# Splitting four head groups instead of two at the end of the first layer, with the schedule's settings chosen anew

## Chip, core and metric

The kernel runs on one core of a Trainium2 chip. The metric is the device time of one execution in microseconds; the engines are TensorE (PE), VectorE (DVE), ScalarE (ACT), GpSimd (POOL) and SyncE (SP), which issues the DMAs.

## What is computed

Two layers, each an attention block and a gated feed-forward block with residual additions, on one sequence of 2048 tokens of width 512, with 32 heads of width 16. The weights of both layers are the same.

```python
def _A_ref(x, wqkv, wo):                       # S=2048, D=512, H=32, Dh=16
    q, k, v = split(x @ wqkv)                  # each (H, S, Dh)
    scores = einsum("bhqd,bhkd->bhqk", q, k) * Dh ** -0.5
    p = softmax(scores)
    return merge(einsum("bhqk,bhkd->bhqd", p, v)) @ wo

def _B_ref(x, w_gate, w_up, w_down):           # hidden width 1792
    return (gelu(x @ w_gate) * (x @ w_up)) @ w_down

x = x + _A_ref(layernorm(x), wqkv, wo)
x = x + _B_ref(layernorm(x), w_gate, w_up, w_down)
x = x + _A_ref(layernorm(x), wqkv, wo)
x = x + _B_ref(layernorm(x), w_gate, w_up, w_down)
```

## The kernel before

**Units.** The queries of a layer are cut into blocks: four of 512 tokens in layer 0, three of 512 and two of 256 in layer 1. Heads are taken in groups of four. One *unit* is one block and one head group. A unit is worked in two passes. The first pass multiplies Q and K, tiles of 128 queries by 512 keys, and takes the maximum of each row (L2440 on PE, L2455 on DVE); a unit of 512 queries has 64 such tiles, and a layer 2048. The maxima go through six small POOL instructions (L1538 to L1543), a transposition on DVE (L1549) and four small DMAs into a spare row of Q's tile (`QT<-MT`). The second pass multiplies K and Q the other way round, so that the maximum is subtracted by the product itself (L2318), takes exponentials on ACT (L2290, table load before the first one after a GELU) and multiplies them with V on PE (L2343), all units in one PSUM bank; a column of ones in V yields the sums. At a unit's end, `nrm` copies the bank on ACT (L1591, tile `ACCS`), and POOL takes the reciprocal and scales (L1597, L1602).

**Folded tiles.** For a part of the first pass, POOL subtracts two quarters of K (L2020, tile `KD`); PE multiplies Q by the difference, ACT takes the positive part (L2270), and one custom instruction on DVE (L2450) then covers two tiles. `want_fold` chooses this when the second pass is close behind the first.

**Dense products.** When all head groups of a block are done, the block's output projection, the layer norm, the three feed-forward products, the next layer's layer norm and its Q, K and V follow. Most are recorded at one helper line (L1235 on PE, `evac` at L1250 on DVE or L1252 on ACT). `x_add` reads a projection out (ACT L1615 and POOL L1617, or DVE L1610). In most blocks the GELU is formed from a tanh, by `gate`, on POOL and ACT (L1743 to L1753), since tanh and the exponential are in one table; in the last block of a layer the gate products are read out by ACT's own GELU function (L1922), which needs a table load, and no exponentials are taken meanwhile. Up products are multiplied in by `L1940`/`L1942`, `L1958`/`L1960` or on DVE (L1952).

**The end of a layer.** The last block of a layer is split: its last `SPL0` head groups in layer 0 (`SPL` in layer 1) are worked by halves of the block, first all of them for half 0, then all of them for half 1, so that half 0's dense products can begin before half 1 is done. Half 0 of layer 0 (256 tokens) takes the tanh way, half 1 the GELU function. The first pass of layer 1 may begin earlier, on the three first quarters of K, for six units; the last quarter of K needs both halves' feed-forward blocks.

```python
k = (SPL if la == NL - 1 else SPL0) if qi == len(sizes) - 1 else 0
if k:
    blocks += [(la, qi, t0, n // 2), (la, qi, t0 + n // 2, n // 2)]
for g in range(NG - k):                     # whole units of the last block
    units.append((la, b, t0, n, g))
for h in range(2 if k else 0):              # then half 0, then half 1
    for g in range(NG - k, NG):
        units.append((la, b + h, t0 + h * n // 2, n // 2, g))
```

**The order of work.** A loop in Python, when the program is built, decides what each engine's stream holds next. It keeps an estimated clock for each engine; in each turn it compares the time at which the next reduction and the next exponential can be fed, and puts dense pieces in between as far as they fit (`lim + over`, where `over` is the setting OV if a chain is past its due place). Where PE's load over the last 3.4 us would fall under a level, it adds filler products on zeros (L2473). Twenty settings steer these choices; the table `PLAN` gives them by steps of the first pass. A step is four tiles, 1024 steps in all, and a row holds until the next key. Among them: OV; LAG, the lag of the second pass behind the first beyond which exponentials get more PSUM banks; LAGT and LAGX, beyond which PSUM is read out by DVE rather than ACT; FL and FX, for the folded tiles; PIECE and GP, the length of dense pieces.

Of the kernel before, what the change touches and what calls it, by code (L numbers as in the profile page):

```python
# [748 lines left out]
def _build(nc, x_in, wqkv, wo, wg, wu, wd, out, layer_blocks=((512, 512, 512, 512), (512, 512, 512, 256, 256)),  # L749
# [16 lines left out]
    with es:  # L766
# [139 lines left out]
        def bank(b):  # L906
            return PS[:, b, :]
# [1796 lines left out]
```

## Time and profile before

| what | us |
|---|---|
| median of three runs | 2457.93 (2454.85 to 2458.28) |
| the profiled execution | 2458.0 |
| its span, first to last instruction | 2456.3 |
| DVE busy | 2388.4 |
| ACT busy | 2321.6 |
| PE busy (filler included) | 2363.2 |
| of it filler (L2473) | 389.8 |
| POOL busy | 1332.0 |

Busy times are sums over the span; a row of instructions gives busy time and the mean of one, and behind the last bar the time in which the engine stood idle just ahead of them, with what ended it. In the order of time of an engine, the first column is the start, the second the length, and a bracket gives idle time before it. The table by stages has one row for each stretch of the span: its length, each engine's busy time with the count of instructions, the granted PE clock, and DMA.

### The profile page before, as it was taken

The numbers are of one execution on the slowest core, as the hardware profiler recorded it, in microseconds if no ns is written. First come the engines' busy times: TensorE is split into PE (matmuls) and PEld (weight loads), VectorE is DVE, ScalarE is ACT, GpSimd is POOL, SyncE is SP. The second block draws the span as 40 slices with busy tenths as digits, with TensorE's granted clock in tenths as the row PEclk, the third lists the DMA queues.
The fourth block names the chain that finished last, engine by engine and source line by source line (L and its number), as shares of the span: only waits on it lengthen the run. The fifth ranks groups of instructions, "written<-read, shape, count | busy, mean of one in ns | idle before, by whom it ended". The sixth has DMA issues, their size and how long they took to land.

```text
span 2456.3 us, 69380 instructions
## 1 busy us (share of the span) xinstructions
PE 2363.2 (96%) x29657; PEld 1152.1 (47%) x29900; DVE 2388.4 (97%) x3217; ACT 2321.6 (95%) x3154; POOL 1332.0 (54%) x2207
## 2 busy tenths in 40 slices
PE   8999999999999999999999999999999999999999
PEld 4444444444444444444543555554444444544456
DVE  9999999999999999999999999999999999999995
ACT  7999999999999999999965999999999999999997
POOL 5111137967579756966572211178427881289372
PEclk9999999999999999999999999999999999999999
DMA  3110000000000000000000000000001000000000
GB/s 95 49 60 9 2 15 13 2 4 13 15 11 4 4 11 20 7 6 21 20 17 16 4 4 4 11 15 2 8 7 21 4 3 11 10 14 6 15 7 13
DMA packets 69477, 35.24 MB, mean 14 GB/s; under 512 B 51504, under 2 KB 68144, under 8 KB 69168
## 3 DMA queue, kind: packets, MB, share of 16 engines
q1 hardware_dynamic: 69168, 30.80, 5.2%
q8 instruction: 234, 3.83, 0.6%
q14 instruction: 75, 0.61, 0.1%
HBM read 9.70 MB, written 2.10 MB: 5 GB/s over the span
## 4 chain that ended last, share of the span: by engine, by line
PE 40%; DVE 39%; ACT 19%; issue 1%; POOL 1%; POOLq 0%; ACTq 0%; DVEq 0%
DVE PM L2455 35%; ACT SCR L2290 17%; PE PS L2440 14%; PE PS L2343 10%; PE PS L1235 9%; PE PS L2318 4%; PE PS L2473 3%; DVE SCR L2450 2%; ACT SCR L2270 1%; DVE HT L1033 0%; PE PS L2263 0%; ACT HT L1252 0%; ACT SCR L1749 0%; DVE AO L2001 0%; DVE HT L1952 0%
## 5 line engine op out<-in xcount | busy, mean ns | idle before, releaser
L2455 DVE TENSOR_REDUCE PM<-PS 128x2 f32<-128x1024 f32 (+1 forms) x2531 | 2182.1, 924 | 31.9 <-PE PS L2318 12.0
L2290 ACT ACTIVATE SCR<-PS 128x1024 bf16<-128x1024 f32 (+1 forms) x2483 | 2014.1, 918 | 67.3 <-PE PS L2318 51.5
L2440 PE MATMUL PS<-KT,QT 32*128 32x512 bf16 x3889 | 1034.6, 385 | 47.2 <-DVE PM L2455 28.8
L2318 PE MATMUL PS<-QT,KT 32*128 32x512 bf16 (+2 forms) x4992 | 921.4, 344 | 2.1 <-ACT SCR L2290 1.3
L2343 PE MATMUL PS<-VP,SCR 128*128 128x51 bf16 (+1 forms) x16384 | 813.9, 187 | 12.4 <-ACT SCR L2290 7.9
L2343 PEld LDWEIGHTS PS<-VP,SCR 128*128 128x128 bf16 x16384 | 576.3, 96 | 504.4 <-issue 425.4
L2440 PEld LDWEIGHTS PS<-KT,QT 32*128 32x128 bf16 x3889 | 246.5, 91 | 512.1 <-DVE PM L2455 304.6
L2473 PE MATMUL PS<-WV,ZER 128*128 128x240 bf16 x2064 | 389.8, 267 | 1.8 <-ACT SCR L2290 0.9
L1597 POOL TENSOR_TENSOR RL<-ACCS,CM 128x16 f32<-128x16 f32 (+2 forms) x68 | 180.3, 2652 | 288.1 <-ACT ACCS L1591 287.7
L2318 PEld LDWEIGHTS PS<-QT,KT 32*128 32x128 bf16 x4992 | 236.7, 91 | 58.4 <-ACT SCR L2290 28.0
L1538 POOL TENSOR_TENSOR PM<-PM 128x32 f32<-128x32 f32 (+2 forms) x78 | 18.7, 240 | 401.3 <-DVE PM L2455 389.7
L2473 PEld LDWEIGHTS PS<-WV,ZER 128*128 128x128 bf16 x2064 | 156.3, 96 | 58.7 <-issue 48.7
L2450 DVE CUSTOM_DVE_ANT_0 SCR<-PS,SCR 128x512 bf16<-128x512 f32 x207 | 132.7, 684 | 3.0 <-PE PS L2440 0.9
L2020 POOL TENSOR_TENSOR KD<-KT 128x512 bf16<-128x512 bf16 x76 | 87.6, 1153 | 72.2 <-PE PS L2263 67.0
L2270 ACT ACTIVATE SCR<-PS 128x1024 bf16<-128x1024 f32 (+1 forms) x104 | 110.4, 1063 | 14.5 <-PE PS L2263 12.3
L1235 PE MATMUL PS<-XNT,WU 128*128 128x512 bf16 (+2 forms) x553 | 118.7, 316 | 5.0 <-issue 2.4
L1235 PE MATMUL PS<-XNT,WG 128*128 128x512 bf16 (+2 forms) x565 | 118.5, 317 | 4.7 <-issue 2.7
L1743 POOL TENSOR_TENSOR SCR<-HT 128x512 bf16<-128x512 bf16 x98 | 101.8, 1039 | 38.8 <-ACT HT L1252 31.4
L1235 PE MATMUL PS<-WD,HT 128*128 128x512 bf16 x387 | 118.4, 381 | 4.1 <-issue 2.2
L1753 POOL TENSOR_TENSOR HT<-HT,SCR 128x512 bf16<-128x512 bf16 x98 | 112.9, 1153 | 4.5
L1747 POOL TENSOR_TENSOR SCR<-SCR,HT 128x512 bf16<-128x512 bf16 x98 | 112.8, 1152 | 1.5
L1617 POOL TENSOR_TENSOR X<-X,AO 128x512 f32<-128x512 f32 x41 | 52.0, 1267 | 90.0 <-ACT AO L1615 89.8
(130 smaller groups left out, 1510.5 us busy)
## 6 DMA issues: line engine op xcount, KB each, us to landing
KT<-SG SPq DMA_DIRECT2D x64, 64.0 KB
QT<-SG SPq DMA_DIRECT2D x54, 64.0 KB
QT<-MT SPq DMA_DIRECT2D x208, 1.0 KB
out_dram<-AO SPq DMA_DIRECT2D x16, 128.0 KB, 1.7
WG<-in_B_w_gate_dram SPq DMA_DIRECT2D x4, 448.0 KB, 4.1
WU<-in_B_w_up_dram SPq DMA_DIRECT2D x4, 448.0 KB, 5.0
WD<-in_B_w_down_dram SPq DMA_DIRECT2D x4, 384.0 KB, 3.6
QT<-MT SPq DMA_DIRECT2D x88, 0.5 KB
```

The lines of the kernel that those rows point to most:

```text
L1235: ins = e.matmul(out_ap, lhsT=l, rhs=r_, start=(i == 0), stop=(i == n - 1))
L1597: emit("pool", lambda e: e.tensor_tensor(RL[:, s, 0:4 * nq], lsum, CM1[:, 0:4 * nq], op=ALU.pow), r=[("ACCS", s), ("CM1",)], w=[("RL", s)] ...
L1747: emit("pool", lambda e: e.tensor_tensor(u, u, ht, op=ALU.mult), r=ku + kh, w=ku, dur=0.18 + n / 520.0)
L1753: emit("pool", lambda e: e.tensor_tensor(ht, ht, u, op=ALU.mult), r=ku + kh, w=kh, dur=0.18 + n / 520.0)
L2270: emit("act", lambda e: e.activation(PT[:, s0:s0 + cnt, :], PS[:, bk:bk + cnt, :], ACTF.Relu), r=bks, w=[("PT", s0 + d) for d in range(cnt ...
L2290: emit("act", lambda e: e.activation(dst, src, ACTF.Exp, scale=DH ** -0.5), r=[BK[bk + i] for i in range(cnt)], w=[("PT", i) for i in slot ...
L2318: ins = e.matmul(bank(bk)[:, i * n:(i + 1) * n], lhsT=KT[32 * j:32 * j + 32, g, kt * 128:(kt + 1) * 128], rhs=QT[32 * j:32 * j + 32, s, c0 ...
L2343: ins = e.matmul(acc, lhsT=PT[:, slot, i * nh + (qt - q0) * 128:i * nh + (qt - q0 + 1) * 128], rhs=AP(VP, (kt * H + 4 * g + j) * 17, [[NTT ...
L2440: ins = e.matmul(bank(b), lhsT=QT[32 * j:32 * j + 32, s, qt * 128:(qt + 1) * 128], rhs=KT[32 * j:32 * j + 32, g, kb * 512:(kb + 1) * 512], ...
L2450: emit("dve", lambda e, i=i, b=b, sl=sl: e.tensor_tensor_reduce(PT[:, sl, :], bank(b), PT[:, sl, :], 1.0, -3.0e38, ALU.add, ALU.max, po[:, ...
L2455: emit("dve", lambda e: e.tensor_reduce(po, PS[:, bs[0]:bs[0] + cnt, :], axis=AX.X, op=ALU.max), r=bks, w=[("PM", sm) + h[1:] for h in hs] ...
L2473: return e.matmul(PS[:, b, NACC:512], lhsT=ZER[:, :], rhs=WV[:, 0, 0:512 - NACC], start=(b != 7), stop=(b != 7), skip_group_check=True)
```

## The change

`SPL0` goes from 2 to 4: in the last block of layer 0, four head groups are worked as whole units, then four as half units of 256 tokens for half 0, then the same four for half 1 (before: six, two and two). That makes 78 units, not 76. The table `PLAN` is replaced: of the 1024 steps, two have the settings that they had. The settings came from a search that weighed dense products done early less than before.

The diff has three more things that are off with their defaults: `LT=0` (layer norms by single tiles, with `i0` the slot), `RCD=0` (a reciprocal on DVE), and packed products in cases where they were single (`PK` over 1; with `PK=1` the packed way is taken in the same blocks, those of 256 tokens with the tanh).

```diff
 PLAN = {
     0: (0.3, 0.25, 0.55, 0.42, 0.0, -0.05, 1, 1, 62, 92, 8, 20, 0.5, 1.5, -10, 18, 1, 3, 7, 92),
+    1: (0.3, 0.05, 0.55, 0.42, 0.0, -0.05, 1, 1, 62, 0, 8, 20, 0.5, 1.5, -10, 18, 1, 3, 7, 92),
+    2: (0.3, 0.05, 0.55, 0.42, 0.0, -0.05, 1, 1, 62, 92, 8, 20, 0.5, 1.5, -10, 18, 1, 3, 7, 92),
...
-    11: (0.3, 0.5, 0.8, 0.22, 0.7, -0.05, 3, 2, 78, 16, 8, 60, 0.1, 4.0, 0, -6, 1, 4, 11, 124),
-    12: (0.3, 0.25, 0.55, 0.42, 0.0, 0.0, 2, 1, 62, 92, 8, 80, 0.5, 1.5, -5, 18, 1, 1, 7, 60),
...
-           ..., FDA=0, SPL0=2, VCH=0, ..., PK=1):
+           ..., FDA=0, SPL0=4, VCH=0, ..., PK=1, LT=0, RCD=0):
...
-            if u_last[u] == len(blocks) - 1:
+            if u_last[u] == len(blocks) - 1 or (RCD and la < NL - 1 and t0 + n == S and g >= NG - 2):
...
-            pk = PK and tg and n == 256
+            pk = PK and (tg or (PK > 1 and not fast)) and n <= 256
+            gs = 512 // n
```

The order of a row of `PLAN` is SPC, SPLIT, S1C, S2C, OV, LIM, NT, P2B, LAG, LAGT, FL, GL, FX, AHD, DUE, DUEM, PIECE, GP, NPV, LAGX. Over the 1024 steps the means go from 0.225 to 0.195 for OV, 39.2 to 46.0 for LAG, 76.3 to 78.5 for LAGT, 84.6 to 76.8 for LAGX, 6.2 to 4.7 for FL, 0.35 to 0.44 for FX, and 2.23 to 2.11 for NT, the most tiles of the second pass put behind one of the first.

More of the change, by code (lines that the diff above doesn't have):

```diff
@@ L749, in _build @@
 def _build(nc, x_in, wqkv, wo, wg, wu, wd, out, layer_blocks=((512, 512, 512, 512), (512, 512, 512, 256, 256)),
-           n_ahead=6, n_pre=6, S1C=0.45, S2C=0.42, OV=0.3, PD=80, FDUE=20, LIM=-0.05, NT=1, AHD=2.0, DUEM=2, FDL2=0, OPD=12, URG=0.3, ft_tok=512, n_pt=8, n_qt=8, SPLIT=0.15, SPC=0.1, PVC=47, WARM=0.55, WARML=0.42, NPV=7, BOOST=0.0, LAG=62, LAGT=84, GP=2, SING=0, DUE=0, END=360, LAGE=10, FD=205, FDL=-10, QD=60, KD_=16, VD=20, FL=8, FMAX=6, NKD=2, FLOOK=2, FX=0.3, GF=0, FAST=1, TG=1, GS=2, P2B=1, PIECE=2, GL=60, GLE=20, HARD=-1e9, LNP=1, LNPT=12, PREO=1, SPL=2, OPL=1, BM=1, LAGB=60, PREO0=1, LNPT0=8, LNPT1=8, QH0=2, QH1=2, OPS=12, FDS=0, FD3=205, FDA=0, SPL0=2, VCH=0, TA=0, TC=0, X3=0, TH=0, HQ=0, TP=1, LAGX=84, G2=0, CAL=0, XD=15, XDT=0.6, XDN=2, PK=1):
+           n_ahead=6, n_pre=6, S1C=0.45, S2C=0.42, OV=0.3, PD=80, FDUE=20, LIM=-0.05, NT=1, AHD=2.0, DUEM=2, FDL2=0, OPD=12, URG=0.3, ft_tok=512, n_pt=8, n_qt=8, SPLIT=0.15, SPC=0.1, PVC=47, WARM=0.55, WARML=0.42, NPV=7, BOOST=0.0, LAG=62, LAGT=84, GP=2, SING=0, DUE=0, END=360, LAGE=10, FD=205, FDL=-10, QD=60, KD_=16, VD=20, FL=8, FMAX=6, NKD=2, FLOOK=2, FX=0.3, GF=0, FAST=1, TG=1, GS=2, P2B=1, PIECE=2, GL=60, GLE=20, HARD=-1e9, LNP=1, LNPT=12, PREO=1, SPL=2, OPL=1, BM=1, LAGB=60, PREO0=1, LNPT0=8, LNPT1=8, QH0=2, QH1=2, OPS=12, FDS=0, FD3=205, FDA=0, SPL0=4, VCH=0, TA=0, TC=0, X3=0, TH=0, HQ=0, TP=1, LAGX=84, G2=0, CAL=0, XD=15, XDT=0.6, XDN=2, PK=1, LT=0, RCD=0):
     S = x_in.shape[1]
@@ L1254, in _build, with ln_fast @@
         ln_cnt = {"n": 0}
-        def ln_fast(tts, x_of, ready, at):
-            for i, tt in enumerate(tts):
+        def ln_fast(tts, x_of, ready, at, i0=0):
+            for i, tt in enumerate(tts, i0):
                 xa, xk = x_of(tt)
@@ L1280, in ln_fast, with ln_head @@
                 at["xn"] = i
-        def ln_head(tts, x_of, ready, at):
-            for i, tt in enumerate(tts):
+        def ln_head(tts, x_of, ready, at, i0=0):
+            for i, tt in enumerate(tts, i0):
                 xa, xk = x_of(tt)
@@ L1302, in ln_head, with ln_pool @@
                 at["xn"] = i
-        def ln_pool(tts, x_of, ready, at):
-            for i, tt in enumerate(tts):
+        def ln_pool(tts, x_of, ready, at, i0=0):
+            for i, tt in enumerate(tts, i0):
                 xa, xk = x_of(tt)
@@ L1371, in transpose_dma, with ln_tile, go @@
             emit("sp", lambda e: e.dma_start_transpose(out=dst_fn, in_=src_fn), r=list(rkeys), w=list(wkeys), grp=grp, nt=XDN, dur=XDT)
-        def ln_to_xnt(tts, tag, ready, due, fast=False):
+        xn_free = [0, 1]
+        mid_wait = [0]
+        def ln_tile(ln, tt, s, tag, ready, due, dma, cnt):
+            at = {"xn": -1, "tr": 9}
+            add(ln([tt], lambda tt: (X[:, tt, :], ("X", tt)), ready, at, s), due)
+            yield ("cond", lambda: at["xn"] >= 0)
+            if ln is ln_pool:
+                locks["SC"] = False
+            if dma:
+                yield ("sp", [("XN", s)], [("XNT", tt)])
+                transpose_dma(XN[:, s, :], [("XN", s)], XNT[:, :, tt * 128:(tt + 1) * 128], [("XNT", tt)], "xt%d" % s)
+            else:
+                yield ("pe", [("XN", s)], [("XNT", tt)])
+                transpose_tile(lambda ck: XN[:, s, ck * 128:(ck + 1) * 128], [("XN", s)],
+                               XNT[:, :, tt * 128:(tt + 1) * 128], [("XNT", tt)])
+            xnt_rec[tt] = tag
+            xn_free.append(s)
+            cnt[0] += 1
+        def ln_to_xnt(tts, tag, ready, due, fast=False):
+            ln = ln_fast if fast else ln_pool if LNP and tts[-1] < (LNPT if tag[0] == "in" else (LNPT0, LNPT1)[tag[1]]) else ln_head
+            if LT:
+                mid = tag[0] == "mid"
+                dma = XD & 1 and not fast and (XD & 4 or tts[-1] < 12 or (mid and tag[1] == NL - 1))
+                cnt = [0]
+                def go():
+                    return bool(xn_free) and not (ln is ln_pool and locks.get("SC")) and not (not mid and mid_wait[0])
+                for tt in tts:
+                    yield ("cond", lambda tt=tt: ready(tt))
+                    mid_wait[0] += mid
+                    while not go():
+                        yield ("cond", go)
+                    mid_wait[0] -= mid
+                    if ln is ln_pool:
+                        locks["SC"] = True
+                    add(ln_tile(ln, tt, xn_free.pop(0), tag, ready, due, dma, cnt), due)
+                yield ("cond", lambda: cnt[0] == len(tts))
+                return
             while locks.get("XN"):
@@ L1377, in ln_to_xnt @@
             at = {"xn": -1, "tr": -1}
-            ln = ln_fast if fast else ln_pool if LNP and tts[-1] < (LNPT if tag[0] == "in" else (LNPT0, LNPT1)[tag[1]]) else ln_head
             add(ln(tts, lambda tt: (X[:, tt, :], ("X", tt)), ready, at), due)
@@ L1887, in ffn, with gemm_p @@
             done = set()
-            pk = PK and tg and n == 256
-            def gemm_p(W, wkey, f0, hk):
-                yield ("pe", xk + [(wkey,)], hk, NCK * n / 2300.0)
+            pk = PK and (tg or (PK > 1 and not fast)) and n <= 256
+            gs = 512 // n
+            def gemm_p(W, wkey, f0, m, hk, run=()):
+                yield ("pe", xk + [(wkey,)], hk, NCK * n / 2300.0) + run
                 b = take_bank()
                 held.add(b)
-                for i in range(2):
+                for i in range(m):
                     if i:
@@ L1900, in gemm_p @@
                 return b
-            for f0 in range(0, NFT if pk else 0, 2):
-                hk = [k for ft in (f0, f0 + 1) for k in ht_keys(ft, h, n)]
-                b = yield from gemm_p(WG, "WG", f0, hk)
-                evac(HV[:, f0:f0 + 2, :], bank(b)[:, 0:2 * n].rearrange("p (a b) -> p a b", a=2), [BK[b]], hk, 2 * n)
-                add(gate(f0, n, due, done, 2, h, True), due)
+            for f0 in range(0, NFT if pk and tg else 0, gs):
+                m = min(gs, NFT - f0)
+                hk = [k for ft in range(f0, f0 + m) for k in ht_keys(ft, h, n)]
+                b = yield from gemm_p(WG, "WG", f0, m, hk)
+                evac(HV[:, f0:f0 + m, :], bank(b)[:, 0:m * n].rearrange("p (a b) -> p a b", a=m), [BK[b]], hk, m * n)
+                add(gate(f0, n, due, done, m, h, True), due)
             for ft in range(NFT if tg and not pk else 0):
@@ L1917, in ffn @@
                 gel["on"] = t0
-            for ft in range(0 if tg else NFT):
+            for f0 in range(0, NFT if pk and not tg else 0, gs):
+                m = min(gs, NFT - f0)
+                hk = [k for ft in range(f0, f0 + m) for k in ht_keys(ft, h, n)]
+                b = yield from gemm_p(WG, "WG", f0, m, hk, ("run",))
+                emit("act", lambda e, b=b, f0=f0, m=m: e.activation(
+                    HV[:, f0:f0 + m, :], bank(b)[:, 0:m * n].rearrange("p (a b) -> p a b", a=m), ACTF.Gelu_apprx_tanh),
+                     r=[BK[b]], w=hk, dur=(1.28 if f0 == 0 and gel["table"] != "gelu" else 0) + 0.055 + m * n / 1200.0)
+            for ft in range(0 if tg or pk else NFT):
                 bgl = []
@@ L1927, in ffn @@
                 gel["table"] = "gelu"
-            for f0 in range(0, NFT if pk else 0, 2):
-                hk = [k for ft in (f0, f0 + 1) for k in ht_keys(ft, h, n)]
-                yield ("cond", lambda f0=f0: f0 in done and f0 + 1 in done)
-                b = yield from gemm_p(WU, "WU", f0, hk)
-                src = bank(b)[:, 0:2 * n].rearrange("p (a b) -> p a b", a=2)
-                dst = HV[:, f0:f0 + 2, :]
+            for f0 in range(0, NFT if pk else 0, gs):
+                m = min(gs, NFT - f0)
+                w = m * n
+                hk = [k for ft in range(f0, f0 + m) for k in ht_keys(ft, h, n)]
+                yield ("cond", lambda f0=f0, m=m: not tg or (f0 in done and f0 + m - 1 in done))
+                b = yield from gemm_p(WU, "WU", f0, m, hk)
+                src = bank(b)[:, 0:w].rearrange("p (a b) -> p a b", a=m)
+                dst = HV[:, f0:f0 + m, :]
                 if fast or pick() == "dve":
                     emit("dve", lambda e, src=src, dst=dst: e.tensor_tensor(dst, src, dst, op=ALU.mult),
-                         r=[BK[b]] + hk, w=hk, dur=0.06 + 2 * n / 963.0)
+                         r=[BK[b]] + hk, w=hk, dur=0.06 + w / 963.0)
                 else:
@@ L1939, in ffn @@
                     ao_cnt["n"] += 1
-                    emit("act", lambda e, b=b, o=o: e.activation(AO[:, o, 0:2 * n], bank(b)[:, 0:2 * n], ACTF.Copy),
-                         r=[BK[b]], w=[("AO", o)], dur=0.055 + 2 * n / 1200.0)
-                    emit("pool", lambda e, dst=dst, o=o: e.tensor_tensor(
-                        dst, dst, AO[:, o, 0:2 * n].rearrange("p (a b) -> p a b", a=2), op=ALU.mult),
-                         r=[("AO", o)] + hk, w=hk, dur=0.18 + 2 * n / 520.0)
+                    emit("act", lambda e, b=b, o=o, w=w: e.activation(AO[:, o, 0:w], bank(b)[:, 0:w], ACTF.Copy),
+                         r=[BK[b]], w=[("AO", o)], dur=0.055 + w / 1200.0)
+                    emit("pool", lambda e, dst=dst, o=o, m=m, w=w: e.tensor_tensor(
+                        dst, dst, AO[:, o, 0:w].rearrange("p (a b) -> p a b", a=m), op=ALU.mult),
+                         r=[("AO", o)] + hk, w=hk, dur=0.18 + w / 520.0)
             for ft in range(0 if pk else NFT):
```

1198 rows, old and new, of the table PLAN are left out of this document.

## The prediction

> **What bounds the kernel now.** I read the page first, then the table of busy time by stages, then ScalarE's order of time around the one stage that stands out.
>
> ```profile
> span 2456.3 us, 69380 instructions
> ...
> PE 2363.2 (96%) x29657; PEld 1152.1 (47%) x29900; DVE 2388.4 (97%) x3217; ACT 2321.6 (95%) x3154; POOL 1332.0 (54%) x2207
> ...
> PEclk9999999999999999999999999999999999999999
> ```
>
> Two engines share the load: DVE takes the row maxima (L2455), ACT the exponentials (L2290), and both are busy nearly from end to end. PE is busy too, but partly with filler (L2473). The profiled execution took 2458.0 us, its span 2456.3 us, so 1.7 us lie outside; the median of the runs shown is 2457.93 us. The sum below is made against 2458.0.
>
> ```profile
> core 0: us, PE busy (x) PEld busy (x) DVE busy (x) ACT busy (x) POOL busy (x), PEclk, DMA share, GB/s
> 0.00:50.00 50.00, 42.55 (x289) 20.89 (x293) 44.16 (x87) 37.64 (x57) 32.05 (x60) 1.00 0.39 117
> 50.00:1200.00 1150.00, 1107.87 (x13881) 528.03 (x13998) 1138.97 (x1518) 1125.53 (x1508) 661.14 (x1139) 1.00 0.06 15
> 1200.00:1350.00 150.00, 143.15 (x1146) 64.29 (x1148) 141.31 (x238) 100.30 (x149) 82.58 (x148) 0.98 0.07 16
> 1350.00:2400.00 1050.00, 1017.63 (x13516) 502.84 (x13618) 1035.99 (x1312) 1019.05 (x1370) 546.40 (x838) 1.00 0.04 9
> 2400.00:2456.30 56.30, 52.04 (x840) 36.04 (x847) 27.98 (x66) 39.04 (x73) 9.85 (x23) 1.00 0.05 14
> ```
>
> The stages say where the two are not busy. DVE is idle 5.8, 11.0, 8.7, 14.0 and 28.3 us in the five rows, ACT 12.4, 24.5, 49.7, 31.0 and 17.3 us: 67.8 us and 134.9 us in all. The largest single piece is ACT's 49.7 us between 1200 and 1350, where the first layer ends and the second begins. The change works exactly there.
>
> ```profile
> 1181.47 0.28 ACT L1591 ACTIVATE ACCS<-PS 128x136 f32<-128x136 f32 x1
> ...
> 1191.06 0.60 ACT L1615 ACTIVATE AO<-PS 128x512 f32<-128x512 f32 x1
> ...
> 1204.37 0.60 ACT L1252 ACTIVATE HT<-PS 128x512 bf16<-128x512 f32 x1 [0.62 <-PE PS L1235]
> ...
> 1218.12 1.02 ACT L2290 ACTIVATE SCR<-PS 128x1024 bf16<-128x1024 f32 x1 [0.76 <-PE PS L2318]
> ...
> 1221.28 0.28 ACT L1591 ACTIVATE ACCS<-PS 128x136 f32<-128x136 f32 x1
> ...
> 1235.58 0.60 ACT L1615 ACTIVATE AO<-PS 128x512 f32<-128x512 f32 x1
> ...
> 1254.81 1.28 ACT L1922 ACT_TABLE_LOAD   x1
> ...
> 1266.44 0.59 ACT L1940 ACTIVATE AO<-PS 128x512 f32<-128x512 f32 x1
> ...
> 1279.59 0.60 ACT L1615 ACTIVATE AO<-PS 128x512 f32<-128x512 f32 x1 [0.77 <-PE PS L1235]
> ...
> 1302.91 0.60 ACT L1615 ACTIVATE AO<-PS 128x512 f32<-128x512 f32 x1 [1.60 <-PE PS L1235]
> ...
> 1319.52 1.28 ACT L2290 ACT_TABLE_LOAD   x1
> 1331.61 1.94 ACT L2290 ACTIVATE SCR<-PS 128x1024 bf16<-128x1024 f32 x2 [10.80 <-PE PS L2318]
> ```
>
> Half 0 of the last block is finished at 1181.47 (copy L1591 of its last unit), half 1 at 1221.28. Half 0's second output projection is read out at 1191.06, its first gate product at 1204.37, its last up product at 1266.44, its second down product at 1279.59. Half 1 follows: 1235.58, then the load of the GELU table at 1254.81 ahead of its gate products, its second down product at 1302.91. Then come layer norm, the last quarter of K and the maxima that needed it; ACT loads the exponential table at 1319.52, waits 10.80 us and has the first exponential of layer 1 at 1331.61. From 1221.28 to that point are 110.3 us without exponentials: the window.
>
> ```profile
> 1000.00:1050.00 50.00, 47.20 (x546) 21.47 (x553) 49.26 (x59) 49.22 (x78) 46.41 (x50) 1.00 0.03 8
> 1150.00:1183.00 33.00, 31.22 (x473) 15.73 (x477) 33.00 (x41) 32.66 (x47) 8.75 (x18) 1.00 0.09 22
> 1183.00:1221.30 38.30, 37.99 (x519) 21.44 (x518) 35.69 (x43) 36.37 (x58) 24.39 (x31) 1.00 0.10 23
> 1221.30:1254.00 32.70, 30.85 (x178) 11.34 (x180) 30.74 (x59) 23.32 (x36) 31.41 (x47) 1.00 0.14 33
> 1221.30:1331.60 110.30, 104.07 (x622) 42.21 (x628) 104.04 (x195) 65.73 (x102) 62.74 (x120) 0.98 0.09 20
> 1320.00:1340.00 20.00, 18.60 (x165) 8.98 (x167) 17.66 (x23) 7.08 (x8) 3.44 (x15) 0.83 0.04 9
> ```
>
> In the window ACT works 65.73 of 110.30 us, so 44.6 us of the 49.7 are here. DVE works 104.04: it reduces tiles of layer 1 ahead of time. In the 70 us before it, DVE, ACT and PE are nearly full.
>
> **The change, part by part.** The code paths that the diff adds for LT, RCD and PK over 1 stay off. What is left is the split of four head groups (SPL0=4) and new settings.
>
> *The split: what moves.* Half 0 now has two more half units behind it. In the trace two half units take 1221.28 - 1181.47 = 39.8 us, so half 0's dense work moves about 37 us earlier against the end of half 1 (I take a little less, because some of the 39.8 was half 0's own dense work). Even at its present pace its last up product then falls at 1229 and its second down product at 1243, instead of 1266 and 1280. Its transposes go to SP's queue at the earlier time, its gates to POOL, which is busy only 8.75 of 33.00 us from 1150 to 1183.
>
> *What half 1's chain gains.* From its last copy to its second projection half 1 needs 14.3 us, half 0 needed 9.6: 4.7 us. From there to the first gate product half 1 needs 19.2 us, half 0 13.3: 5.9 us. In that stretch POOL is busy 31.41 of 32.70 us with half 0's gates, and half 1's normalisation and additions queue behind them. Third, half 0's two down products run on PE between half 1's GELUs and its up products.
>
> ```profile
> L1235 PE MATMUL PS<-XNT,WU 128*128 128x256 bf16 x112 | 15.6, 274 | 0.1
> L1235 PE MATMUL PS<-WD,HT 128*128 128x512 bf16 x53 | 14.0, 381 | 0.4 <-issue 0.3
> ...
> L1235 PE MATMUL PS<-XNT,WG 128*128 128x256 bf16 x56 | 7.8, 274 | 0.0
> ```
>
> WD's 53 recorded matmuls are both halves', so half 0's part is 7.0 us. Together 17.6 us, so the window shrinks from 110.3 to 92.7 us. The bounds are 0 (half 1 is slow by itself) and 36: 4.7 + 5.9, and the stretch from 1254.81 to 1302.91 (48.1 us) down to PE's dense work in it, 7.8 + 7.8 + 7.0 = 22.6 us. I take 17.6 because half 0 itself ran at that pace in the first two steps.
>
> *What the move costs.* The ACT work of half 0 that lay in the window now lies before it, where ACT is full, and delays the last exponential by as much.
>
> ```profile
> L2270 ACT ACTIVATE SCR<-PS 128x1024 bf16<-128x1024 f32 x31 | 31.7, 1023 | 11.2 <-PE PS L2263 9.4 <-PE PS L2440 1.6
> ...
> L1615 ACT ACTIVATE AO<-PS 128x512 f32<-128x512 f32 x6 | 3.6, 596 | 2.9 <-PE PS L1235 2.4 <-PE PS L2440 0.4
> L1940 ACT ACTIVATE AO<-PS 128x512 f32<-128x512 f32 x6 | 3.6, 595 | 2.7 <-PE PS L1235 2.7
> L1749 ACT ACTIVATE SCR<-SCR 128x512 bf16<-128x512 bf16 x4 | 2.5, 624 | 0.0
> ```
>
> That is four tanh (L1749), six up copies (L1940) and two of the six additions (L1615): 2.5 + 3.6 + 1.2 = 7.3 us. So the idle time that ACT saves is 17.6 - 7.3 = 10.3 us (bounds: -7.3 and 28.7).
>
> *What saved ACT time is worth.* DVE is the fuller engine, so ACT's time only counts if work can pass from DVE to ACT. It can, by the folded tiles: ACT forms a rectified difference of two tiles (L2270), DVE then needs one custom instruction in place of a tile of its reduction.
>
> ```profile
> L2455 DVE TENSOR_REDUCE PM<-PS 128x2 f32<-128x1024 f32 x631 | 764.9, 1216 | 11.9 <-PE PS L2440 4.5 <-PE PS L2318 3.7 <-PE PS L2263 0.4
> L2455 DVE TENSOR_REDUCE PM<-PS 128x1 f32<-128x512 f32 x682 | 459.1, 680 | 3.4 <-PE PS L2318 1.6 <-PE PS L2440 0.2
> L2450 DVE CUSTOM_DVE_ANT_0 SCR<-PS,SCR 128x512 bf16<-128x512 f32 x188 | 120.4, 684 | 2.8 <-PE PS L2440 0.9 <-PE PS L2263 0.5 <-PE PS L2318 0.3
> ...
> L1549 DVE STREAM_TRANSPOSE MT<-MSEL 128x32 bf16<-128x32 bf16 x35 | 7.1, 202 | 0.0
> ```
>
> One L2270 (1.02 us) replaces two wide reductions (2 x 1.216) by two customs (2 x 0.684): DVE saves 1.06 us. With ACT's y us free, x folds balance at 1.06 x = y - 1.02 x, so the time falls by 0.51 y: 5.3 us, from +3.7 to -14.6 us at the bounds. If no folds pass, it is 0.
>
> *Instructions added.* Four half units stand where two whole ones stood: two more copies of sums on ACT, at most 0.28 us each by the row at 1221.28, and two more transposes on DVE at 0.20: shared between the two, +0.5 us. Two more projections of Q, two more sets of small DMAs and two more powers and differences on POOL and SP lie beside other work; uncovered, a unit's exponentials would wait for its maxima as at 1319.52, some 10.8 us, but only if DVE were no unit ahead.
>
> *The settings.* Of the 1024 steps two keep their settings. The mean allowance by which an overdue dense piece may hold up PE (OV) falls from 0.225 to 0.195 us, the lag beyond which exponentials take the reductions' banks (LAG) rises from 39 to 46 tile pairs, the lag limit of folds (FL) falls from 6.2 to 4.7 and their preference (FX) rises from 0.35 to 0.44. None has a row. The bound is the idle time that they steer, that of the two long stages: 25.0 us of DVE and 55.5 of ACT. All of it gained, shared between the two, would be 40 us; nothing says it cannot rise by a quarter, 10 us, as well. I take -4 us, a tenth of what there is, since OV is the setting whose direction is plain: fewer dense pieces ahead of a due reduction.
>
> [...] The clock row, 1320 to 1340, shows 0.83 granted, at the point where PE waits for the last of K; elsewhere it is 1.00. [...]
>
> *The sum.* 2458.0 - 5.3 + 0.5 - 4.0 = 2449.2, so 2449 us.
>
> **Rivals.** *The cover is gone (slower).* Half 0's products, 22.6 us of PE, must now run before 1221, and PE is the third full engine there.
>
> ```profile
> 1150.00:1183.00 33.00, 5.56 (x27) 2.09 (x27) 1.00 0.09 22
> 1183.00:1221.30 38.30, 3.45 (x21) 1.73 (x21) 1.00 0.10 23
> ```
>
> Filler to be displaced is 5.56 + 3.45 = 9.0 us, idle PE 1.8 + 0.3 = 2.1 us. What is beyond 11.1 us, 11.5 us, would hold up reductions and exponentials alike: 2458.0 + 11.5 - 5.3 + 0.5 = 2465 us. It decides once more than 5 us of it find no room. Against it: from 1000 to 1050 POOL is 46.41 us busy with gates, so dense work runs there, while DVE (49.26) and ACT (49.22) stay full. For it: those 50 us are not the 70 just before the window, where PE has 37.99 of 38.30.
>
> *Nothing gained.* Half 1's chain is slow by itself, or the folds do not follow: +3.7 to 0 for the window, +0.5, settings 0: 2458 to 2462 us. For it: of the 288 tiles of layer 1 that can be reduced before the last of K (six units, 48 each), 2 x 631 + 682 + 2 x 188 - 2048 = 272 are done by 1317.2. DVE uses the window fully already, and its 67.8 us idle change little.
>
> *Late dense work (slower).* Products put off in layer 1 could pile up after 2400, where DVE has 28.3 of 56.3 us idle and nothing covers them: each us open there is a us of time. With 10 us late: 2458.0 + 10 - 5.3 + 0.5 = 2463 us.
>
> *More than that.* Window at its bound of 36 us: 2458.0 - 14.6 + 0.5 - 4.0 = 2440 us; with settings at -7, 2437.
>
> [...]
>
> **How the numbers follow.** Forecast 0.45 (its own range 2443 to 2453), more than that 0.13, nothing gained 0.14, second dip 0.03, cover gone 0.15, late dense work 0.10. 0.2% is 4.9 us, about what a measurement of this kernel can tell: below 2453 is faster, above 2463 slower. Faster: 0.45 + 0.13 = 0.58. Same: 0.14 + 0.03 = 0.17. Slower: 0.15 + 0.10 = 0.25. The range of eight in ten reaches from the bound 2437 to 2466, which takes in both slower rivals at their prices.
>
> **What would show it.** In the profile of the changed kernel: half 0's last copy some 75 us, not 40, before half 1's; its second down product read out before half 1's GELU table load; from half 1's last copy to the first exponential of layer 1 about 93 us, not 110; ACT idle there about 34 us, not 45; and more custom instructions on DVE than before. PE filler before the window near 0 and DVE waiting for PE there would show the lost cover. Wrong altogether would be a window as long as before with a time far from 2458: then the settings, not the split, decide.

## The result, and the profile after

The changed kernel takes 2442.65 us (median of six runs, 2441.59 to 2445.65), before 2457.44 us: ratio 0.9938, 95% interval 0.9921 to 0.9954, so 15 us or 0.6% faster. The profiled execution took 2441.87 us, its span is 2440.2 us.

Line numbers behind the new table differ: L1591 is now L1704 (a unit's copy), L1615 is L1728 (a projection or down product read out), L1922 is L2044 (GELU), L1235 is L1309 (dense products), L2290 is L2414 (exponentials), L2270 is L2394 (folds), L2450 is L2574 (their custom instruction). The page, and the table by stages (length, then busy time of PE, weight loads, DVE, ACT, POOL):

```profile
span 2440.2 us, 69860 instructions
...
PE 2380.9 (98%) x29929; PEld 1149.2 (47%) x29929; DVE 2382.1 (98%) x3203; ACT 2326.3 (95%) x3275; POOL 1351.0 (55%) x2232
```

```profile
0.00:50.00 50.00, 44.09 (x289) 20.62 (x289) 43.74 (x86) 37.23 (x57) 32.04 (x60) 0.97 0.39 117
50.00:1200.00 1150.00, 1125.85 (x14158) 534.75 (x14158) 1144.41 (x1521) 1129.20 (x1568) 687.22 (x1178) 1.00 0.06 15
1200.00:1350.00 150.00, 144.30 (x1233) 61.02 (x1231) 146.30 (x253) 109.05 (x156) 66.50 (x138) 1.00 0.09 19
1350.00:2400.00 1050.00, 1029.71 (x13672) 506.38 (x13671) 1033.15 (x1301) 1025.83 (x1445) 562.55 (x853) 1.00 0.04 9
2400.00:2440.30 40.30, 36.92 (x590) 26.39 (x586) 14.55 (x47) 25.04 (x52) 2.74 (x5) 1.00 0.06 18
```

DVE's idle time goes from 5.8, 11.0, 8.7, 14.0, 28.3 us to 6.3, 5.6, 3.7, 16.9, 25.8 us: 9.7 us less. ACT's in the stage from 1200 to 1350 goes from 49.7 to 41.0 us. DVE's busy time falls by 6.3 us. ACT in order of time (start, length):

```profile
1144.37 0.29 ACT L1704 ACTIVATE ACCS<-PS 128x136 f32<-128x136 f32 x1
...
1222.27 0.28 ACT L1704 ACTIVATE ACCS<-PS 128x136 f32<-128x136 f32 x1
...
1245.08 0.59 ACT L1728 ACTIVATE AO<-PS 128x512 f32<-128x512 f32 x1
1246.73 0.60 ACT L1728 ACTIVATE AO<-PS 128x512 f32<-128x512 f32 x1 [1.06 <-PE PS L1309]
...
1258.43 1.28 ACT L2044 ACT_TABLE_LOAD   x1
...
1293.77 0.60 ACT L1728 ACTIVATE AO<-PS 128x512 f32<-128x512 f32 x1 [4.08 <-PE PS L1309]
...
1312.18 1.28 ACT L2414 ACT_TABLE_LOAD   x1
1319.65 1.94 ACT L2414 ACTIVATE SCR<-PS 128x1024 bf16<-128x1024 f32 x2 [6.19 <-PE PS L2442]
```

Half 0's last copy is now 77.9 us before half 1's, and the window without exponentials lasts from 1222.27 to 1319.65, 97.4 us, not 110.3. ACT loads a table four times in this execution, at 0.79, 1258.43, 1312.18 and 2417.05 us, 1.28 us each; between the third load and the fourth it takes 49 tanhs (L1862) among 1294 exponentials without another load. With these marks the 16.1 us of the two spans split up: half 1's last copy 1.0 us later, the window 12.9 us shorter, layer 1 from its first exponential to the last GELU table load 3.9 us shorter (1101.3 to 1097.4), the end after that load 0.3 us shorter.

Some 2 of the 12.9 us belong to the one execution of before that was profiled. Its granted clock was 0.83 from 1320 to 1340 us. Experiment e4 below issues the same instructions in the same order on DVE and ACT up to 1980 us; its execution kept the clock at 1.00, and its window is 2.2 us shorter:

```profile
1224.82:1332.95 108.13, 101.89 (x621) 41.55 (x627) 103.78 (x194) 65.76 (x102) 62.79 (x120) 1.00 0.09 21
```

At equal clock the window therefore falls from 108.1 to 97.4 us, by 10.7.

### The profile page after: what moved, and what is told of

It is laid out like the page before. It is cut to its first block, busy times and chain, and to the rows that moved or that the text cites. A ratio compares the mean times of both kernels' runs of the same rounds, so it can differ in the third digit from the quotient of the medians.

```text
span 2440.2 us, 69860 instructions
## 1 busy us (share of the span) xinstructions
PE 2380.9 (98%) x29929; PEld 1149.2 (47%) x29929; DVE 2382.1 (98%) x3203; ACT 2326.3 (95%) x3275; POOL 1351.0 (55%) x2232
## 4 chain that ended last, share of the span: by engine, by line
PE 44%; DVE 39%; ACT 16%; issue 1%; POOL 0%; DMA 0%; SPq 0%; ACTq 0%; POOLq 0%; DVEq 0%
DVE PM L2579 36%; PE PS L2564 15%; ACT SCR L2414 14%; PE PS L2467 11%; PE PS L1309 10%; PE PS L2442 4%; PE PS L2597 4%; DVE SCR L2574 2%; ACT SCR L1862 0%; PE PS L2387 0%; ACT AO L2082 0%; ACT SCR L2394 0%; ACT HT L1326 0%; ACT SG L1326 0%; DVE AO L2125 0%
## 5 line engine op out<-in xcount | busy, mean ns | idle before, releaser
L2414 ACT ACTIVATE SCR<-PS 128x1024 bf16<-128x1024 f32 (+1 forms) x2590 | 2021.9, 886 | 51.6 <-PE PS L2442 34.9
L2442 PE MATMUL PS<-QT,KT 32*128 32x512 bf16 (+2 forms) x5120 | 934.3, 340 | 2.2 <-ACT SCR L2414 1.0
L2597 PE MATMUL PS<-WV,ZER 128*128 128x240 bf16 x1961 | 370.7, 265 | 0.1
L2597 PEld LDWEIGHTS PS<-WV,ZER 128*128 128x128 bf16 x1961 | 149.3, 96 | 55.6 <-issue 50.6
L1309 PE MATMUL PS<-WD,HT 128*128 128x512 bf16 x448 | 138.9, 381 | 0.2 <-ACT AO L1728 0.2
L1309 PE MATMUL PS<-XNT,WU 128*128 128x512 bf16 (+2 forms) x616 | 138.6, 323 | 0.5 <-ACT SCR L2394 0.3
L1309 PE MATMUL PS<-XNT,WG 128*128 128x512 bf16 (+2 forms) x616 | 137.3, 323 | 0.3 <-DVE XNT L1324 0.3
L2084 POOL TENSOR_TENSOR HT<-HT,AO 128x512 bf16<-128x512 bf16 (+1 forms) x96 | 104.3, 1089 | 45.0 <-ACT AO L2082 43.8
L2574 DVE CUSTOM_DVE_ANT_0 SCR<-PS,SCR 128x512 bf16<-128x512 f32 x197 | 126.1, 684 | 0.6 <-PE PS L2564 0.2
L2394 ACT ACTIVATE SCR<-PS 128x1024 bf16<-128x1024 f32 x99 | 104.5, 1056 | 13.7 <-PE PS L2387 8.9
```

The source lines that it names most:

```text
L1309: ins = e.matmul(out_ap, lhsT=l, rhs=r_, start=(i == 0), stop=(i == n - 1))
L2394: emit("act", lambda e: e.activation(PT[:, s0:s0 + cnt, :], PS[:, bk:bk + cnt, :], ACTF.Relu), r=bks, w=[("PT", s0 + d) for d in range(cnt ...
L2414: emit("act", lambda e: e.activation(dst, src, ACTF.Exp, scale=DH ** -0.5), r=[BK[bk + i] for i in range(cnt)], w=[("PT", i) for i in slot ...
L2442: ins = e.matmul(bank(bk)[:, i * n:(i + 1) * n], lhsT=KT[32 * j:32 * j + 32, g, kt * 128:(kt + 1) * 128], rhs=QT[32 * j:32 * j + 32, s, c0 ...
L2574: emit("dve", lambda e, i=i, b=b, sl=sl: e.tensor_tensor_reduce(PT[:, sl, :], bank(b), PT[:, sl, :], 1.0, -3.0e38, ALU.add, ALU.max, po[:, ...
L2597: return e.matmul(PS[:, b, NACC:512], lhsT=ZER[:, :], rhs=WV[:, 0, 0:512 - NACC], start=(b != 7), stop=(b != 7), skip_group_check=True)
```

## Experiments

Three theories stood against each other: the split shortens the window and that is the gain; the new settings are better and that is the gain; or the settings fit one exact sequence of decisions and any other sequence is worse. In each table below "window" runs from half 1's last copy to the first exponential of layer 1, "layer 1" from there to the last load of the GELU table.

### One part of the change alone, and a small disturbance

```diff
e1: SPL0=4, PLAN of before              e2: SPL0=2, PLAN of after
e3: after, OV + 0.01 in every row       e4: before, OV + 0.01 in every row
```

> The split of four head groups with the settings of before. Split theory: the window from half 1's last copy to the first exponential of layer 1 falls from 110 us to about 97, as in the changed kernel, and the time to about 2448 us (ratio 0.996), less what settings chosen for another order of units lose. Settings theory: the time stays at 2457 us or above, since the settings are those of before. Scatter theory: anywhere from 2450 to 2475, with a window that has nothing to do with the time.

> The new settings with the split of two head groups. Split theory: the window is 110 us or more again, half 0's dense products lie in it, and the time is 2452 us or more; layer 0 ends (half 1's last copy) up to 7 us earlier than in the changed kernel, because less dense work lies ahead of it. Settings theory: 2443 us, as the changed kernel, with a window of any length. Scatter theory: 2450 to 2475 us.

> The changed kernel with the allowance OV raised by 0.01 us in every row, so that decisions differ a little throughout and nothing else changes. Split and settings theories, if the settings are good as a whole: within 5 us of the changed kernel, 2440 to 2448 us. Scatter theory: the settings fit one exact sequence of decisions, and off it the time is 8 us or more worse, 2450 us and above. The window stays near 97 us by the split theory in any case.

> The kernel before with OV raised by 0.01 us in every row. It gives the yardstick for the first two: if the settings are good as a whole, 2453 to 2462 us; by the scatter theory 8 us or more above 2457. The window stays near 110 us by the split theory.

| kernel | us | ratio to before (95%) | half 1's last copy | window | layer 1 |
|---|---|---|---|---|---|
| before | 2457.4 | | 1221.3 | 110.3 | 1101.3 |
| after | 2442.65 | 0.9938 (0.9921 to 0.9954) | 1222.3 | 97.4 | 1097.4 |
| e1, split alone | 2486.85 | 1.0115 (1.0096 to 1.0134) | 1235.6 | 109.3 | 1117.3 |
| e2, settings alone | 2521.2 | 1.0262 (1.0237 to 1.0286) | 1232.7 | 110.0 | 1149.0 |
| e3, after, OV + 0.01 | 2470.8 | 1.0054 (1.0036 to 1.0072) | 1222.5 | 97.4 | 1125.2 |
| e4, before, OV + 0.01 | 2470.5 | 1.0056 (1.0033 to 1.0078) | 1224.8 | 108.1 | 1114.4 |

Each part alone makes the kernel slower, by 29 and 64 us; both lie above the 2450 to 2475 us that the third theory had given them. A hundredth of a microsecond in one setting costs 28 us on the new kernel and 13 us on the old one. Where e3 loses them shows in the stages; the changed kernel's layer 1 first (the row ends 0.85 us before its last table load), then e3's window and layer 1:

```profile
1319.65:2416.20 1096.55, 1075.04 (x14385) 531.14 (x14385) 1066.73 (x1348) 1067.61 (x1493) 569.20 (x875) 1.00 0.04 9
```

```profile
1222.47:1319.86 97.39, 92.21 (x539) 34.98 (x544) 94.74 (x189) 62.51 (x97) 42.96 (x99) 1.00 0.11 23
1319.86:2445.10 1125.24, 1083.08 (x14330) 536.84 (x14447) 1078.63 (x1367) 1070.13 (x1489) 562.53 (x868) 1.00 0.04 9
```

The window agrees with the changed kernel's to 0.01 us. In layer 1 DVE is idle 46.6 us instead of some 30, ACT 55.1 instead of some 29, and DVE is busy some 11 us longer. The disturbance reaches less far than was expected: instruction by instruction, e3's order on DVE and ACT is the changed kernel's up to 1700 us, and e4's is that of before up to 1980 us. Nothing in layer 0 changes, and all of the loss comes after the first decision that turns out differently. So the third theory holds in the main: what one calls the settings is a list of decisions that fit, and off the list 13 to 64 us are lost. The windows of the split alone and of the settings alone,

```profile
1235.60 0.29 ACT L1630 ACTIVATE ACCS<-PS 128x136 f32<-128x136 f32 x1
...
1275.71 1.28 ACT L1970 ACT_TABLE_LOAD   x1
...
1344.94 1.94 ACT L2340 ACTIVATE SCR<-PS 128x1024 bf16<-128x1024 f32 x2 [9.46 <-PE PS L2368]
```

```profile
1232.69 0.28 ACT L1704 ACTIVATE ACCS<-PS 128x136 f32<-128x136 f32 x1
...
1267.18 1.28 ACT L2044 ACT_TABLE_LOAD   x1
...
1342.73 1.02 ACT L2414 ACTIVATE SCR<-PS 128x1024 bf16<-128x1024 f32 x1 [2.44 <-PE PS L2442]
```

are 109.3 and 110.0 us: with the settings of before the split does not shorten the window, though the split theory said that it would. With the old settings the step up to the GELU load takes 40.1 us, with two groups and the new ones 34.5.

### What in the window is whose

```diff
e5: - OPS=12     + OPS=-300      # half 1's output projection due ahead of half 0's down products
e6: + if la == 0 and h == 0: ... ffn_rec[tt] = la; return   # ffn: half 0 of layer 0 without its block
```

> The changed kernel with half 1's output projection of layer 0 due ahead of half 0's down products (OPS=-300), settings unchanged. Queue theory (in the changed kernel half 1's second projection waits for half 0's 28 down products on PE): the second projection is read out about 10 us after half 1's last copy, not 24; half 0's down products then move behind it, between 0 and 10 us of the window are saved. Rival (the planner's order hardly matters, since half 1's layer norms and the products of V set the pace): the window stays within 3 us of 97. The total is likely worse than 2443 us, since the settings were chosen for the other order.

> The changed kernel without half 0's feed-forward block in layer 0 (256 tokens keep only their attention part, so that block's products, gates and additions are left out). It shows what of the window is half 1's own chain. Step of the prediction (half 0's work costs half 1 time in the window): with it gone the window falls to some 85 us or less. Rival (half 1's chain is slow by itself, through its layer norms, its small tiles and the products of V): 92 to 97 us.

In the changed kernel's order of PE, half 1's first output projection is followed by half 0's two down products; the second projection comes after them:

```profile
1233.19 1.03 PE L1309 MATMUL PS<-WO,ATTT 128*128 128x512 bf16 x4
...
1234.91 1.04 PE L1309 MATMUL PS<-WD,HT 128*128 128x512 bf16 x4 [0.15 <-ACT AO L1728]
...
1243.95 0.61 PE L1309 MATMUL PS<-WD,HT 128*128 128x512 bf16 x2
...
1245.24 0.60 PE L1309 MATMUL PS<-WO,ATTT 128*128 128x512 bf16 x2 [0.36 <-ACT SCR L2394]
```

In e5 both projections stand first (PE, then ACT):

```profile
1231.81 1.04 PE L1309 MATMUL PS<-WO,ATTT 128*128 128x512 bf16 x4
...
1233.67 1.03 PE L1309 MATMUL PS<-WO,ATTT 128*128 128x512 bf16 x3
...
1239.02 0.59 PE L1309 MATMUL PS<-WD,HT 128*128 128x512 bf16 x2
...
1247.81 1.04 PE L1309 MATMUL PS<-WD,HT 128*128 128x512 bf16 x4
```

```profile
1222.74 0.28 ACT L1704 ACTIVATE ACCS<-PS 128x136 f32<-128x136 f32 x1
...
1234.73 0.60 ACT L1728 ACTIVATE AO<-PS 128x512 f32<-128x512 f32 x1 [0.34 <-PE PS L1309]
...
1250.79 1.28 ACT L2044 ACT_TABLE_LOAD   x1
...
1314.42 1.02 ACT L2414 ACTIVATE SCR<-PS 128x1024 bf16<-128x1024 f32 x1 [2.44 <-PE PS L2442]
```

The second projection is read out 12.0 us after the last copy (24.5 in the changed kernel), the GELU table is loaded after 28.1 us (36.2), and the window is 91.7 us. So 8.1 us are won up to the load, 2.4 of them are lost again behind it, and 5.7 remain. Only the due time of half 1's projections was changed, though the loop decided anew all that follows. The total was 2490.87 us in one run; layer 1 took 1148.6 us, since its settings belong to another sequence. Without half 0's block (one run, 2482.43 us, with less work in it and no fit either):

```profile
1216.54 0.29 ACT L1704 ACTIVATE ACCS<-PS 128x136 f32<-128x136 f32 x1
...
1240.97 1.28 ACT L2049 ACT_TABLE_LOAD   x1
...
1302.90 1.02 ACT L2419 ACTIVATE SCR<-PS 128x1024 bf16<-128x1024 f32 x1 [6.40 <-PE PS L2447]
```

The window is 86.4 us and the GELU load comes after 24.4 us, near the 85 us of the first expectation. That is half 1's chain without half 0's block. By this measure half 0's work costs the window some 11 us in the changed kernel. Before it cost 22 (at the clock of e4) to 24 us, if half 1's chain was as long there, which was not measured.

### The split at equal fit

To compare two and four groups fairly, both got the new settings up to step 432, ahead of the first place where they differ, and from there the rows of before, improved by one and the same short search on the planner's own clocks; two draws of random numbers. Last, both were run with no table at all.

```diff
e7, e8: SPL0=2 and 4, PLAN refitted from step 432, draw 1
e9, e10: the same, draw 2
e11, e12: SPL0=2 and 4, PLAN = {}
```

> Split of two head groups, after's settings up to step 432 (ahead of the first place where the splits differ), and from there on settings chosen anew: from before's rows, the same search for both splits, 16 random candidate rows at every fourth step, kept if the planner's own clocks end earlier. First of two draws. Split theory: window about 110 us, time some 5 to 10 us above its partner with four. Fit theory (only the fit of the settings counts): within 3 us of its partner, window either way.

> Its partner: split of four head groups, same rows up to step 432, same search, same random numbers. Split theory: window 92 to 100 us, 5 to 10 us faster than the two. Fit theory: within 3 us of it. Both above the changed kernel, whose settings were searched for longer.

> As the first with two head groups, second draw of random numbers. Split theory: window about 110 us, time within 5 us of the first draw. Fit theory: draws of one split differ by as much as the splits.

> As the first with four head groups, second draw. Split theory: window 92 to 100 us, 5 to 10 us faster than both draws with two. Fit theory: draws of one split differ by as much as the splits.

> Split of two head groups with no table of settings: the constants of the function's head at every step. Fit theory: 2500 us or more, since nothing is fitted. Its window should be near 110 us if the window belongs to the split.

> The same with four head groups. Split theory, if its 4 to 8 us hold under any settings: 4 to 8 us faster than the two, with a window near 100 us. Fit theory: the difference of the two is lost in the scatter of unfitted sequences, some 10 us either way; the window may still be shorter.

| kernel | us (runs) | ratio to before (95%) | last copy | window | layer 1 |
|---|---|---|---|---|---|
| e7, two, draw 1 | 2465.2 (10) | 1.0024 (1.0013 to 1.0035) | 1229.8 | 108.0 | 1101.9 |
| e8, four, draw 1 | 2461.3 (10) | 1.0008 (0.9997 to 1.0019) | 1234.2 | 103.8 | 1101.9 |
| e9, two, draw 2 | 2465.7 (10) | 1.0028 (1.0018 to 1.0037) | 1227.9 | 117.7 | 1094.6 |
| e10, four, draw 2 | 2457.8 (10) | 0.9996 (0.9987 to 1.0006) | 1231.9 | 99.2 | 1101.5 |
| e11, two, no table | 2541.7 (2) | 1.0329 (1.0296 to 1.0362) | 1268.6 | 110.3 | 1135.2 |
| e12, four, no table | 2548.2 (2) | 1.0355 (1.0322 to 1.0388) | 1279.1 | 104.8 | 1135.3 |

The ends of the window, two and four groups, by draws and without a table:

```profile
1229.76 0.28 ACT L1628 ACTIVATE ACCS<-PS 128x136 f32<-128x136 f32 x1
...
1337.76 1.94 ACT L2338 ACTIVATE SCR<-PS 128x1024 bf16<-128x1024 f32 x2 [8.62 <-PE PS L2366]
```

```profile
1234.21 0.28 ACT L1619 ACTIVATE ACCS<-PS 128x136 f32<-128x136 f32 x1 [0.43 <-PE PS L2382]
...
1337.96 1.94 ACT L2329 ACTIVATE SCR<-PS 128x1024 bf16<-128x1024 f32 x2 [4.09 <-PE PS L2357]
```

```profile
1227.92 0.28 ACT L1624 ACTIVATE ACCS<-PS 128x136 f32<-128x136 f32 x1
...
1345.66 1.94 ACT L2334 ACTIVATE SCR<-PS 128x1024 bf16<-128x1024 f32 x2 [3.11 <-PE PS L2362]
```

```profile
1231.87 0.29 ACT L1623 ACTIVATE ACCS<-PS 128x136 f32<-128x136 f32 x1
...
1331.11 1.94 ACT L2333 ACTIVATE SCR<-PS 128x1024 bf16<-128x1024 f32 x2 [6.19 <-PE PS L2361]
```

```profile
1268.58 0.28 ACT L1063 ACTIVATE ACCS<-PS 128x136 f32<-128x136 f32 x1
...
1378.86 1.94 ACT L1773 ACTIVATE SCR<-PS 128x1024 bf16<-128x1024 f32 x2 [8.75 <-PE PS L1801]
```

```profile
1279.08 0.28 ACT L1063 ACTIVATE ACCS<-PS 128x136 f32<-128x136 f32 x1
...
1383.89 1.94 ACT L1773 ACTIVATE SCR<-PS 128x1024 bf16<-128x1024 f32 x2 [8.98 <-PE PS L1801]
```

At equal search four groups are 3.9 and 7.9 us faster; the two intervals of the first pair overlap a little, those of the second do not. Scatter in layer 1 does not explain this: from about 1380 us on, the order on DVE and ACT in all four is that of before but for a few instructions. The windows of e8 (103.8 us, expected 92 to 100) and e9 (117.7, expected about 110) missed, and so did the first pair's gain (expected 5 to 10 us). The two draws with two groups lie within 0.5 us of each other, those with four within 3.5. Without a table four groups are 6.5 us slower: the window is 5.5 us shorter, but half 1's last copy comes 10.5 us later. Half 0's up products, 13.1 us of PE, now lie in front of it, and from 1150 us to the last copy PE is busy 126.8 of 129.1 us, in e11 114.6 of 118.6. So the split was worth 4 to 8 us in two draws, and cost 6 without a table. Of the 15 us of the change 7 to 11 us are left for the settings' fit; that is a subtraction and not a measurement. The whole table is worth some 85 to 105 us (e11 against before, e12 against after). The short search did not fit either split well: with two groups it ends some 8 us above the kernel before, with four 15 to 19 us above the changed one. Two draws are few, and a longer search could move either number; that stays open. None of the variants beat the changed kernel.

## Why the prediction was right, and where not

*Direction and place.* Faster was forecast, by 8.8 us to 2449, with a range of 2437 to 2466. It is 2442.65, 15 us faster: inside the range, and just below the 2443 to 2453 of the forecast itself. The window did shrink, half 0's last copy is 77.9 us ahead (75 was expected), its second down product is read out at 1245 (1243), and ACT's idle time in the window is 34.8 us (34.3).

*The window's size: two steps wrong, in opposite directions.* The first two steps, from the last copy to the second projection and from there to the GELU load, were to gain 4.7 + 5.9 us, down to 22.9 us. They take 36.2 us, 2.6 more than before. The reason given, POOL full of half 0's gates, does not decide it: in the changed kernel POOL works 18.47 of the 31.70 us behind the last copy, against 31.41 of 32.70, and the piece is no shorter. What decides is PE's order: half 0's down products, moved out of the third piece, landed between half 1's two projections; e5 takes them out and gets 8.1 us back in this piece. There it takes 28.1 us, 5.5 less than before, about half of what was forecast; how much of that is POOL's is open. The third piece, from the load to the second down product, was to gain 7.0 us, PE's time for these products; it gains 12.8 (48.1 to 35.3 us). The last piece, held constant in the sum, gains 2.8 us, of which 2.2 are the slow clock in before's execution. Together 12.9, or 10.7 at equal clock, against 17.6; e6 leaves 22 to 24 us as the most to be had in such an order, not 36.

*The cost of the move.* 7.3 us were expected as a later last copy. The pairs show 10.5 without a table, 4.5 in draw 1 and 4.0 in draw 2. In the draws part of it comes from the start of the execution (last section): at 862 us, up to where both programs have one order on ACT, the kernel with four groups is 2.7 and 1.2 us behind. That leaves 1.8 and 2.7 us for the move. Right in kind; its size is the settings' matter.

*What ACT's time is worth: wrong.* Folds were to carry work from DVE to ACT. There are fewer of them, not more; folds on ACT and custom instructions on DVE, before and after:

```profile
L2270 ACT ACTIVATE SCR<-PS 128x1024 bf16<-128x1024 f32 (+1 forms) x104 | 110.4, 1063 | 14.5 <-PE PS L2263 12.3 <-PE PS L2440 1.6
...
L2450 DVE CUSTOM_DVE_ANT_0 SCR<-PS,SCR 128x512 bf16<-128x512 f32 x207 | 132.7, 684 | 3.0 <-PE PS L2440 0.9 <-PE PS L2263 0.5 <-PE PS L2318 0.3
```

```profile
L2394 ACT ACTIVATE SCR<-PS 128x1024 bf16<-128x1024 f32 x99 | 104.5, 1056 | 13.7 <-PE PS L2387 8.9 <-DVE PM L2574 3.0 <-PE PS L2564 1.2
...
L2574 DVE CUSTOM_DVE_ANT_0 SCR<-PS,SCR 128x512 bf16<-128x512 f32 x197 | 126.1, 684 | 0.6 <-PE PS L2564 0.2 <-PE PS L2442 0.2
```

With 10 custom instructions fewer, DVE reduces 20 more single tiles (1400 instead of 1380, 0.68 us each), 14 us against 7. It was relieved elsewhere by as much: 11 fewer up products of 512 columns are multiplied on it, 7 us. The lengths of all its instructions add up to 2604 and 2605 us in the two traces; they overlap more, so that it is busy 6.3 us less, and it is idle 9.7 us less. And the factor 0.51 does not hold: in draw 1 and without a table the order of layer 1 is the same for both splits but for its first 40 us, layer 1 lasts the same to 0.1 us, and the shorter window counts in full. In draw 2, 18.5 us of window come with 6.9 us more in layer 1, so 0.63 counts. This error and the overrated window pull in opposite directions; that they nearly meet is luck.

*The settings: right by luck.* -4 us, bounded at 10 us of loss, was argued from the mean of OV. A shift of OV by a third of the change in its mean (0.01 of 0.03) loses 13 to 28 us. The step that failed is the bound itself: DVE's idle time in e3's layer 1 rises by some 16 us, not by 10 at most, and idle time is not all that settings can lose, since they also decide what DVE has to do (e3: some 11 us more busy time there).

*The rivals.* The lost cover did not happen in the changed kernel: from 50 us to the last copy DVE waits less than before (5.6 us instead of 11.0 up to 1200). It did happen without a table: 10.5 us later, close to the 11.5 us worked out, and the net loss of 6.5 us close to its 6.7 (11.5 - 5.3 + 0.5). Late dense work: the end after the last GELU load takes 23.1 us, as before. A second clock dip, to which the chances give 0.03, did not come: from 1200 to 1350 us the changed kernel's granted clock is 1.00, and PE's longest idle stretch in the window is 0.41 us. The dip of before is gone as well. There the granted clock was 0.50 from 1326.2 to 1333.0 us, and in the 16 us ahead of that no idle stretch of PE was longer than 0.74 us. e4's execution, with the order of before, has a granted clock of 1.00 through its window, so the order of work alone does not bring the dip about. No run shows what does: the 0.03 was the author's estimate, and the cause stays open.

## To carry to other kernels

Where a long table of scheduling choices was searched for one program, take no part of a change out of it and measure it alone: disturb the table first, by next to nothing, and see how far the time moves; here 13 to 28 us, where the change itself is worth 15. A structural change is compared at equal fit, both sides searched alike, with more than one draw. Two windows are compared at equal granted clock. And when work is moved off one step of a chain, look in the queue of the engine that runs it for the step on which it lands.

## What was not expected of the hardware

The first 50 us differ between executions of one program order. The changed kernel, e2, e3 and e5 to e10 have the same order of instructions on ACT up to 853 us. Still the 56th of these instructions begins between 47.96 and 52.20 us. The spread follows the granted clock of the first 50 us: about 48.0 us where it is 1.00 (e2, e9), 48.4 to 49.3 us where it is 0.97, 52.2 us where it is 0.90 (e6, e8). The stage row of e8:

```profile
0.00:50.00 50.00, 42.97 (x269) 21.94 (x274) 40.52 (x79) 34.55 (x53) 30.37 (x51) 0.90 0.39 117
```

ACT has begun 53 instructions there, in the changed kernel's row at 0.97 it has begun 57. So up to 4.2 us of a single execution's time are settled at the start, which is why e7 and e8 are compared by medians of ten runs and not by their profiled executions (2465.13 and 2465.09 us). Beyond that these executions keep step: at 853 us the nine still lie within 4.3 us of each other, and e3 and the changed kernel are 0.2 us apart at 1320 us.
